# Small second-layer tiles multiply the weights where they arrived, and the first layer of 144 and 160 tokens moves both parts of x in one matmul

## The chip, the cores and the metric

One core of one Trainium2 chip. The metric is the device time of one execution in microseconds (us). The kernel before takes 419.78 us (median of 3 runs, 419.25 to 420.67).

## The reference

Attention over a window of 64 positions, then a mixture of eight experts over the 4608 resulting rows of 512 numbers. A row whose skip score is not positive is passed through; every other row goes to the one expert with the highest logit.

```python
x = attention(q, k, v)                      # 4608 x 512
do = x @ w_skip > 0
e = argmax(x[do] @ w_gate); g = softmax(x[do] @ w_gate)[e]
h = maximum(x[do] @ w1[e], 0)               # first layer, 512 -> 1024
out[do] = x[do] + g * (h @ w2[e])           # second layer, 1024 -> 512
out[~do] = x[~do]
```

All tensors are float32.

## The kernel before, in words

The attention runs to about 164 us and is not touched. Behind and partly beside it run the experts, as ten **items** in a fixed order, each a number of tokens of one expert: 256, 256, 144, 368, 336, 288, 256, 240, 160 and 112. The work of this text is in the third (item 2, 144 tokens; it uses the same weights as item 1) and in the ninth (item 8, 160 tokens). Item 9 (112 tokens) is the last.

**Precision by parts.** Each matrix is split in a high part, which TensorE takes in its fast format, and the low part that is left over. A product is then three matmuls: `mm3` (L911 to L913) issues high by high, high by low and low by high into one PSUM tile.

**Weights.** 72 pieces of 512 KB (128 x 1024) come by DMA from SP's queue (`weight_dma`, L834) into one of six `raw` buffers. `weight_split` makes the high part on ScalarE (`whi`, L843) and the low part on VectorE (`wlo`, L847, which reads `raw` and `whi`) into a ring of nine pairs. `weights_to` issues transfers and splits ahead of their use.

**Steps.** Every item has four steps of a quarter of the 1024 hidden numbers (`qi`). In step k of the list `steps`, `expert_chunks` issues the first layer of step k (`up`) and then the second layer of step k-2 (`down`), so an item's own second layer starts in its third step, and the first two steps of an item hold the last second-layer work of the item before. Splits of weights are issued between these pieces, so ScalarE and VectorE, which work in program order, get them between the small operations of `up`.

**First layer.** `up` works in two halves (`f` = 0, 1) of 128 hidden numbers. One half is four blocks of the contraction, each one `mm3` with 128 x 128 weights and n tokens as the moving columns, into the PSUM tile `p1` (two buffers, so a half can start only when the half before the last has been read). ScalarE then writes the high part of the ReLU (`hh`, L957) and, for items with a small last tile, a plain copy of its last tokens (`hp`, L959); VectorE writes the low part (`hl`, L960). For item 9 (one tile) the roles of weights and tokens are exchanged and there is a buffer `hs` (L970) with one slot.

**Second layer.** `down` multiplies 128 tokens of `hh` and `hl` by the weights, 512 columns, by `mm3`. When the last tile of an item has at most 32 rows (16 in item 2, 32 in items 5 and 8) it is done by `down_small` instead: plain float32 matmuls of `hp` by an unsplit copy of the same weights, `wr`, which `load_plain` (L978 to L982) brings by DMA a second time, 24 transfers of 256 KB in all, in four buffers. After an item's fourth `down`, `finish` writes its rows (`yo`, L994) on VectorE.

**Tokens of the next item.** While one item runs, the next one's tokens are transposed on TensorE into the PSUM tile `px` (one buffer), and split by ScalarE (`xh`, L889) and VectorE (`xl`, L892). A three-tile item has its tiles split behind the second half of step 1, the second half of step 2 and the first half of step 3 of the item before it; a one-tile item behind the first half of step 3.

Of the kernel before, what the change touches and what calls it, by code (L numbers as in the profile page):

```python
# [8 lines left out]
F32 = mybir.dt.float32  # L9
# [56 lines left out]
OOB = 1 << 20  # L66
NWR = 4
XN = max(n for _, n, _ in ITEMS)
# [75 lines left out]
def window_attention_moe(ctx: ExitStack, tc, a, out):  # L144
# [683 lines left out]
    def weight_dma(n):  # L828
        e, qi, w = pieces[n]
        if e not in wrow:  # L830
            r = e % E
            ix = perm[0:1, r : r + 1] if r < 2 else tables["order"][0:1, r : r + 1]
            wrow[e] = nc.values_load(ix, engines=[SP], min_val=0, max_val=(E - 1) * NQ * P)
        nc.sync.dma_start(  # L834
            raws[n % NRAW], a["wq"][bass.ds(wrow[e] + qi * P, P), w * 1024 : w * 1024 + 1024]
        )
# [5 lines left out]
    def weight_hi(n):  # L842
        nc.scalar.copy(ring[n % RING][0], raws[n % NRAW])  # L843

    def weight_lo(n, by):
        hi, lo = ring[n % RING]
        by.tensor_tensor(lo, raws[n % NRAW], hi.bitcast(F32), op=ALU.subtract)  # L847

# [4 lines left out]
    def weights_to(n):  # L853
        n = min(n, len(pieces), ptr["free"] + len(ring))
        while ptr["split"] < n:
            while ptr["dma"] < min(len(pieces), ptr["split"] + NRAW):
                if not can_load(ptr["dma"]):
                    break
                weight_dma(ptr["dma"])
                ptr["dma"] += 1  # L860
            if ptr["dma"] == ptr["split"]:
                break
            weight_split(ptr["split"])
            ptr["split"] += 1
        while ptr["dma"] < min(len(pieces), ptr["split"] + NRAW) and can_load(ptr["dma"]):
            weight_dma(ptr["dma"])
            ptr["dma"] += 1
# [3 lines left out]
    def can_load(n):  # L871
        return pieces[n][0] % E < 2 or "order" in tables
# [42 lines left out]
    class Item:  # L915
        def __init__(self, n, e=None):
            self.e = e
            self.n, self.nt = n, -(-n // P)
            self.rows = [min(P, n - j * P) for j in range(self.nt)]
            self.small = self.nt > 1 and self.rows[-1] <= 32  # L920
            self.hh, self.hl, self.hp, self.wr = {}, {}, {}, {}

# [8 lines left out]

        def split(self, xh, xl, j, px=None):
# [11 lines left out]
    def up(it, qi, wh, wl):  # L944
# [6 lines left out]
        if nt > 1:  # L951
            for f in range(2):
                p1 = psum.tile([P, n], F32, name="p1", tag="t", bufs=2, padded_shape=[P, 512])
                for c in range(NDC):
                    w = slice(c * FQ + f * P, c * FQ + f * P + P)
                    mm3(p1, wh[:, w], wl[:, w], *it.xc[c], c == 0, c == NDC - 1)
                nc.scalar.activation(hh[:, f], p1, AF.Relu)  # L957
                if it.small:
                    nc.scalar.activation(hp[:, f, : it.rows[-1]], p1[:, n - it.rows[-1] :], AF.Relu)  # L959
                pace[0] = nc.vector.scalar_tensor_tensor(  # L960
                    hl[:, f], p1, 0.0, hh[:, f].bitcast(F32), op0=ALU.max, op1=ALU.subtract
                )
                yield 0.65 * nt
        else:
# [11 lines left out]
            nc.vector.tensor_tensor(hl, pt[:, :, :n], hh.bitcast(F32), op=ALU.subtract)  # L976

    def load_plain(it, h):  # L978
        if h < 2 * NQ:
            it.wr[h] = wr = hpool["y"].tile([P, D], F32, name="wr", bufs=NWR)  # L980
            c = 1024 + h % 2 * D
            nc.sync.dma_start(wr, a["wq"][bass.ds(wrow[it.e] + h // 2 * P, P), c : c + D])  # L982

# [31 lines left out]
    def down_small(it, qi, y, m):  # L1015

        for f in range(2):
            h = 2 * qi + f
            for z in range(4):
                nc.tensor.matmul(  # L1020
                    y[32 * z : 32 * z + m, 0:P],
                    it.hp[qi][:, f, :m],
                    it.wr[h][:, z * P : (z + 1) * P],
                    start=h == 0,
                    stop=h == 2 * NQ - 1,
                    skip_group_check=True,
                )
            load_plain(it, h + NWR)

# [90 lines left out]
    with tc.manual_schedule():  # L1120
# [341 lines left out]
```

## Time and profile before

| | before |
|---|---|
| median of 3 runs | 419.78 us |
| lowest and highest run | 419.25 and 420.67 us |
| the profiled execution's own time | 421.82 us |
| its span, first to last instruction | 420.0 us |
| granted TensorE clock | 0.999 of full speed |
| TensorE busy (PE) | 395.7 us, 94% |
| weight loads of TensorE (PEld) | 332.5 us, 79% |
| VectorE busy (DVE) | 291.2 us, 69% |
| ScalarE busy (ACT) | 219.4 us, 52% |
| moved by DMA | 105.71 MB |

The profile is of one execution. A row of the timeline gives the start in us, the duration, engine, line, operation, the tile written and the tiles read, the shape, how many instructions the row holds, and in brackets how long the engine was idle before it and what released it. Rows overlap a little: on every engine the next instruction begins before the end of the one before it.

### The profile page before, as it was taken

How to read it: one execution, taken by the hardware profiler on the slowest of the kernel's cores; microseconds unless marked ns; L12 is line 12 of the kernel's file. 1: busy time of each engine (PE TensorE's matmuls, PEld its weight loads, DVE VectorE, ACT ScalarE, POOL GpSimd, SP SyncE). 2: the span in 40 equal slices, each digit the busy share in tenths (PEclk: the TensorE clock that was granted, in tenths of full speed). 3: DMA queues.
4: the chain of work that ended last, by engine and by line, in shares of the span. 5: the costliest groups of instructions: out<-in, count | busy, mean ns of one | idle time of the engine just before them, and what ended most of it. 6: DMA issues, size and time to landing. Idle time of an engine off the chain costs nothing.

```text
span 420.0 us, 11720 instructions
## 1 busy us (share of the span) xinstructions
PE 395.7 (94%) x4679; PEld 332.5 (79%) x4679; DVE 291.2 (69%) x514; ACT 219.4 (52%) x388; POOL 159.1 (38%) x297
## 2 busy tenths in 40 slices
PE   4998999999999898889999899999999999999994
PEld 3576878878778677779988789888888889988873
DVE  2497889899799796999426569754554675656661
ACT  0676767777767694526224426334424455444540
POOL 5211158656958878477103006004006030100110
PEclk9999999999999999999999999999999999999999
DMA  7999999999997695646838845547388866567710
GB/s 259 386 338 346 410 377 336 407 411 282 386 413 248 198 358 163 210 154 192 305 94 264 262 148 205 201 153 241 101 251 269 273 208 216 193 221 237 267 62 21
DMA packets 38841, 105.71 MB, mean 252 GB/s; under 512 B 4896, under 2 KB 6816, under 8 KB 38784
## 3 DMA queue, kind: packets, MB, share of 16 engines
q1 hardware_dynamic: 34160, 93.51, 65.0%
q0 software_dynamic: 3200, 9.58, 6.4%
q10 hardware_dynamic: 1424, 1.85, 1.3%
q8 instruction: 37, 0.61, 0.6%
q14 instruction: 20, 0.16, 0.1%
HBM read 90.86 MB, written 14.39 MB: 251 GB/s over the span
## 4 chain that ended last, share of the span: by engine, by line
PE 62%; issue 12%; DMA 10%; DVE 6%; POOL 5%; ACT 2%; POOLq 0%; ACTq 0%; SPq 0%; DVEq 0%
PE p L911 7%; PE p L913 7%; PE av L388 7%; PE p L912 6%; PE pt L285 6%; PE ps L252 5%; DMA out<-yo,les 5%; DMA vTt<-vTt 3%; PE yv L911 3%; PE yv L912 3%; PE yv L913 3%; PE pw L336 2%; PE yw L911 2%; PE ps L238 2%; PE yw L912 2%
## 5 line engine op out<-in xcount | busy, mean ns | idle before, releaser
L847 DVE TENSOR_TENSOR wlo<-raw,whi 128x1024 fp32r<-128x1024 f32 x70 | 86.9, 1252 | 18.0 <-ACT whi L843 16.9
L957 ACT ACTIVATE hh<-p 128x256 fp32r<-128x256 f32 (+6 forms) x72 | 27.8, 386 | 128.0 <-PE p L913 119.3
L911 PE MATMUL p<-xh,whi 128*128 128x256 f32 (+6 forms) x288 | 85.2, 296 | 1.2 <-ACT xh L889 0.9
L912 PE MATMUL p<-xl,whi 128*128 128x256 f32 (+6 forms) x288 | 83.7, 290 | 0.9 <-DVE xl L892 0.9
L913 PE MATMUL p<-xh,wlo 128*128 128x256 f32 (+6 forms) x288 | 83.7, 291 | 0.6 <-DVE wlo L847 0.6
L843 ACT CAST whi<-raw 128x1024 fp32r<-128x1024 f32 x72 | 74.4, 1048 | 0.0
L1003 POOL DMA_INDIRECT out<-yo,les x18 | 17.6, 977 | 149.7 <-DVE yo L994 139.7
L960 DVE SCALAR_TENSOR_TENSOR hl<-p,hh 128x256 fp32r<-128x256 f32 (+6 forms) x72 | 30.1, 420 | 61.8 <-ACT hh L957 30.0
L911 PEld LDWEIGHTS p<-xh,whi 128*128 128x128 f32 x288 | 54.5, 189 | 4.9 <-issue 1.5
L912 PEld LDWEIGHTS p<-xl,whi 128*128 128x128 f32 x288 | 54.5, 189 | 2.2 <-DVE xl L892 1.2
L913 PEld LDWEIGHTS p<-xh,wlo 128*128 128x128 f32 x288 | 54.5, 189 | 0.8 <-DVE wlo L847 0.8
L277 ACT ACTIVATE s<-s 128x1024 f32<-128x1024 f32 x36 | 38.1, 1059 | 26.2 <-DVE s L272 26.0
L271 DVE TENSOR_REDUCE mx<-ps 128x8 f32<-128x1024 f32 x36 | 43.6, 1211 | 10.8 <-PE ps L252 10.8
L272 DVE TENSOR_TENSOR s<-ps,mx 128x1024 f32<-128x1024 f32 x36 | 44.1, 1225 | 5.0 <-ACT vt L373 0.5
L388 PEld LDWEIGHTS av<-vm,ptm 128*64 128x64 f32 x992 | 34.5, 136 | 11.5 <-issue 5.0
L388 PE MATMUL av<-vm,ptm 128*64 128x74 f32 x992 | 39.6, 230 | 2.6 <-POOL vm L357 1.5
L286 ACT COPY ptm<-pt 128x512 f32<-128x512 f32 x72 | 38.3, 582 | 7.0 <-PE pt L285 6.9
L285 PE MATMUL pt<-ident,s 128*128 128x128 f32 x288 | 39.2, 279 | 1.1 <-issue 1.1
L252 PE MATMUL ps<-k,q 64*64 64x128 f32 x1024 | 35.9, 279 | 2.9 <-DMA q<-qT 2.9
L252 PEld LDWEIGHTS ps<-k,q 64*64 64x64 f32 x1024 | 31.8, 138 | 6.5 <-DMA q<-qT 2.7
L285 PEld LDWEIGHTS pt<-ident,s 128*128 128x128 f32 x288 | 30.9, 141 | 3.7 <-issue 1.5
L357 POOL COPY vm<-vm 64x1184 f32<-64x1184 f32 x16 | 18.7, 1167 | 33.0 <-ACT vm L356 28.8
(224 smaller groups left out, 696.3 us busy)
## 6 DMA issues: line engine op xcount, KB each, us to landing
raw<-wq SPq DMA_DIRECT2D x72, 512.0 KB
vm<-vp SPq DMA_DIRECT2D x15, 592.0 KB
vT<-vT SPq DMA_DIRECT2D x16, 512.0 KB
out<-x SPq DMA_DIRECT2D x32, 256.0 KB
q<-qT SPq DMA_DIRECT2D x14, 512.0 KB
wr<-wq SPq DMA_DIRECT2D x24, 256.0 KB
k<-kT SPq DMA_DIRECT2D x7, 640.0 KB
k<-kT SPq DMA_DIRECT2D x7, 512.0 KB
```

What stands on the lines that cost most here:

```text
L252: nc.tensor.matmul(ps[64 * hf : 64 * hf + 64, r, p], q[h, p], k[h, :, p], start=False, stop=p == 3, skip_group_check=True,)
L271: nc.vector.tensor_reduce(mx, flat, axis=AX.X, op=ALU.max)
L272: pace[0] = nc.vector.tensor_tensor(s, flat, mx.unsqueeze(2).to_broadcast([P, 8, P]), op=ALU.subtract)
L277: nc.scalar.activation(s, s, AF.Exp, scale=0.125)
L285: nc.tensor.transpose(pt[:, p], s[:, 4 * r + p], ident)
L286: nc.scalar.copy(ptm[:, 4 * r : 4 * r + 4], pt)
L388: nc.tensor.matmul(av[64 * hf : 64 * hf + 64, h // 4, (h % 4) * VW : (h % 4 + 1) * VW], ptm[:, (h % 2) * 4 + h // 2, 64 * hf : 64 * hf + 6 ...
L843: nc.scalar.copy(ring[n % RING][0], raws[n % NRAW])
L847: by.tensor_tensor(lo, raws[n % NRAW], hi.bitcast(F32), op=ALU.subtract)
L911: nc.tensor.matmul(o, lh, rh, start=first, stop=False, skip_group_check=parts)
L912: nc.tensor.matmul(o, lh, rl, start=False, stop=False, skip_group_check=parts)
L913: nc.tensor.matmul(o, ll, rh, start=False, stop=last, skip_group_check=parts)
```

## The change

It has two parts. In the first, `load_plain` and the `wr` buffers go. `down_small` reads the weights in the `raw` buffer in which they arrived; such a buffer is held until `down_small` has read it, and two more `raw` buffers (eight instead of six) are handed out from a list of idle ones. In the second, items with more than 128 and at most 160 tokens (items 2 and 8) keep the high and the low part of x side by side in one tile. Per block, one matmul moves both parts through the weights' high part (288 or 320 columns, into the two parts of `p1`), and a second one moves the high part of x through the weights' low part into the second part of `p1`. The two parts of `p1` are then added: ScalarE copies the second part to SBUF (`rest`, in the buffer `hs`), VectorE adds the first part to it in place, and `hh`, `hp` and `hl` are made from that sum.

```diff
-NWR = 4
+PAIRED = 160
+MORERAW = 2
...
+    idle, raw_of = list(raws), {}
+    plain = {e for _, n, e in ITEMS if P < n and 0 < n % P <= 32}
+    held_raw = lambda n: pieces[n][2] == 1 and pieces[n][0] in plain
...
+        raw_of[n] = idle.pop(0)
         nc.sync.dma_start(
-            raws[n % NRAW], a["wq"][bass.ds(wrow[e] + qi * P, P), w * 1024 : w * 1024 + 1024]
+            raw_of[n], a["wq"][bass.ds(wrow[e] + qi * P, P), w * 1024 : w * 1024 + 1024]
         )
...
     def weight_lo(n, by):
         hi, lo = ring[n % RING]
-        by.tensor_tensor(lo, raws[n % NRAW], hi.bitcast(F32), op=ALU.subtract)
+        by.tensor_tensor(lo, raw_of[n], hi.bitcast(F32), op=ALU.subtract)
+        if not held_raw(n):
+            idle.append(raw_of.pop(n))
...
-            while ptr["dma"] < min(len(pieces), ptr["split"] + NRAW):
+            while ptr["dma"] < len(pieces) and idle:
...
+            self.pairs = [pair[:, c, :, : self.n] for c in range(NDC)] if P < self.n <= PAIRED else None
...
-                    mm3(p1, wh[:, w], wl[:, w], *it.xc[c], c == 0, c == NDC - 1)
+                    if it.pairs:
+                        nc.tensor.matmul(
+                            p1, wh[:, w], it.pairs[c], start=c == 0, stop=False, skip_group_check=True
+                        )
+                        nc.tensor.matmul(
+                            p1[:, n:], wl[:, w], it.xc[c][0],
+                            start=False, stop=c == NDC - 1, skip_group_check=True,
+                        )
+                    else:
+                        mm3(p1, wh[:, w], wl[:, w], *it.xc[c], c == 0, c == NDC - 1)
+                if it.pairs:
+                    rest = pool.tile([P, FQ], F32, name="hs")[:, :n]
+                    nc.scalar.copy(rest, p1[:, n:])
+                    nc.vector.tensor_tensor(rest, p1[:, :n], rest, op=ALU.add)
+                    p1 = rest
                 nc.scalar.activation(hh[:, f], p1, AF.Relu)
...
     def down_small(it, qi, y, m):
+        n = when[it.e, qi, 1]
...
-                    it.wr[h][:, z * P : (z + 1) * P],
+                    raw_of[n][:, f * D + z * P : f * D + (z + 1) * P],
...
-            load_plain(it, h + NWR)
+        idle.append(raw_of.pop(n))
...
+        for s in "12":
+            pair = mr.tile([P, NDC, 2, XN], F32R, name=f"xp{s}")
+            xhl.append((pair[:, :, 0], pair[:, :, 1], pair))
         ring_slots(mr, RING - len(ring))
+        idle.extend(mr.tile([P, 1024], F32, name=f"raw{NRAW + i}") for i in range(MORERAW))
```

The order of instructions on an engine is fixed when the program is built; the rows below are of that order, each with the engines or queues whose semaphores it waits for (PE, DVE, Activation; DMAHW is a DMA queue of SP, DMASW one of POOL).

ScalarE in item 8, its first two halves. Before:

```order
L957 ACTIVATE hh<-p_5546 128x160 [waits DVE_49,PE_49]
L959 ACTIVATE hp<-p_5546 128x32
L843 CAST whi_3374<-raw_134 128x1024 [waits DMAHW5_49]
L957 ACTIVATE hh<-p_5565 128x160 [waits PE_49]
L959 ACTIVATE hp<-p_5565 128x32
L843 CAST whi_3376<-raw_135 128x1024 [waits DMAHW6_49]
```

and with the change:

```order
L977 COPY hs<-p_5507 128x160 [waits PE_49]
L980 ACTIVATE hh<-hs 128x160 [waits DVE_49]
L982 ACTIVATE hp<-hs 128x32
L848 CAST whi_3372<-raw_136 128x1024 [waits DMAHW5_49]
L977 COPY hs<-p_5524 128x160 [waits DVE_49,PE_49,Activation_49]
L980 ACTIVATE hh<-hs 128x160 [waits DVE_49]
L982 ACTIVATE hp<-hs 128x32
L848 CAST whi_3374<-raw_3377 128x1024 [waits DMAHW6_49]
```

The copy and the VectorE sum now stand ahead of the ReLU `hh`, and so ahead of the next `whi`.

VectorE at the end of item 8 (`hs` written by L978 is the sum; `xl`, now the second half of the tile `xp`, is that of item 9). Before:

```order
L960 SCALAR_TENSOR_TENSOR hl<-p_5731,hh 128x160 [waits DVE_49,PE_49,Activation_49]
L847 TENSOR_TENSOR wlo_3265<-raw_134,whi_3264 128x1024 [waits DMAHW3_49,Activation_49]
L892 TENSOR_TENSOR xl_3367<-px_5749,xh_3366 128x4x112 [waits Activation_49]
L960 SCALAR_TENSOR_TENSOR hl<-p_5756,hh 128x160 [waits Activation_49]
L847 TENSOR_TENSOR wlo_3371<-raw_135,whi_3370 128x1024 [waits DMAHW4_49,Activation_49]
```

and with the change:

```order
L978 TENSOR_TENSOR hs<-p_5673,hs 128x160 [waits Activation_49]
L983 SCALAR_TENSOR_TENSOR hl<-hs,hh 128x160 [waits Activation_49]
L852 TENSOR_TENSOR wlo_3265<-raw_138,whi_3264 128x1024 [waits DMAHW3_49,Activation_49]
L899 TENSOR_TENSOR xp_3366<-px_5690,xp_3366 128x4x112 [waits Activation_49]
L978 TENSOR_TENSOR hs<-p_5697,hs 128x160 [waits Activation_49]
L983 SCALAR_TENSOR_TENSOR hl<-hs,hh 128x160 [waits Activation_49]
L852 TENSOR_TENSOR wlo_3369<-raw_3377,whi_3368 128x1024 [waits DMAHW4_49,Activation_49]
```

Each sum stands behind the `wlo` of the half before it, and the last one also behind the `xl` of item 9; before, only `hl` stood there.

VectorE in the third step of item 2 (`yo` finishes item 1, `xl` or `xp` is the second tile of item 3). Before:

```order
L847 TENSOR_TENSOR wlo_3375<-raw_137,whi_3374 128x1024 [waits DMAHW0_49,Activation_49]
L847 TENSOR_TENSOR wlo_3377<-raw_138,whi_3376 128x1024 [waits DMAHW1_49,Activation_49]
L994 SCALAR_TENSOR_TENSOR yo<-yv,es_114,xg_117 128x512 [waits DMASW2_49,PE_49]
L994 SCALAR_TENSOR_TENSOR yo<-yv,es_114,xg_118 128x512 [waits DMASW3_49,DMASW1_49,PE_49]
L960 SCALAR_TENSOR_TENSOR hl<-p_4015,hh 128x144 [waits DVE_49,Activation_49]
L960 SCALAR_TENSOR_TENSOR hl<-p_4031,hh 128x144 [waits Activation_49]
L892 TENSOR_TENSOR xl_3367<-px_4047,xh_3366 128x4x128 [waits Activation_49]
```

and with the change:

```order
L852 TENSOR_TENSOR wlo_3373<-raw_3376,whi_3372 128x1024 [waits DMAHW0_49,Activation_49]
L852 TENSOR_TENSOR wlo_3375<-raw_3377,whi_3374 128x1024 [waits DMAHW1_49,Activation_49]
L1011 SCALAR_TENSOR_TENSOR yo<-yv,es_114,xg_117 128x512 [waits DMASW2_49,PE_49]
L1011 SCALAR_TENSOR_TENSOR yo<-yv,es_114,xg_118 128x512 [waits DMASW3_49,DMASW1_49,PE_49]
L978 TENSOR_TENSOR hs<-p_3991,hs 128x144 [waits Activation_49]
L983 SCALAR_TENSOR_TENSOR hl<-hs,hh 128x144 [waits Activation_49]
L978 TENSOR_TENSOR hs<-p_4006,hs 128x144 [waits Activation_49]
L983 SCALAR_TENSOR_TENSOR hl<-hs,hh 128x144 [waits Activation_49]
L899 TENSOR_TENSOR xp_3366<-px_4021,xp_3366 128x4x128 [waits Activation_49]
```

The two sums stand where the two `hl` stood, behind two `wlo` and two `yo`.

## Rows read from the trace of the kernel before

**Rows 1.** The page: busy us, share of the span and instructions of TensorE and others.

```profile
PE 395.7 (94%) x4679; PEld 332.5 (79%) x4679; DVE 291.2 (69%) x514; ACT 219.4 (52%) x388; POOL 159.1 (38%) x297
```

**Rows 2.** Waits of TensorE from 188 to 412 us: total, times, longest.

```profile
PE p L911 <- ACT xh L889: 0.9, 1, 0.9
PE p L912 <- DVE xl L892: 0.9, 1, 0.9
```

**Rows 3.** Windows, item 8: length, busy of PE, PEld, DVE, ACT, POOL, PEclk, DMA share, GB/s.

```profile
376.10:397.00 20.90, 20.90 (x169) 18.18 (x169) 12.68 (x20) 11.01 (x25) 1.94 (x2) 1.00 0.82 265
```

**Rows 4.** Timeline of TensorE at the start of item 2, behind a 512-column matmul.

```profile
212.33 0.23 PE L911 MATMUL p<-xh,whi 128*128 128x144 f32 x1
212.40 0.28 PE L912 MATMUL p<-xl,whi 128*128 128x144 f32 x1
212.51 0.28 PE L913 MATMUL p<-xh,wlo 128*128 128x144 f32 x1
```

**Rows 5.** Timeline of TensorE in item 5, 288 columns.

```profile
314.04 0.29 PE L911 MATMUL p<-xh,whi 128*128 128x288 f32 x1
314.17 0.30 PE L912 MATMUL p<-xl,whi 128*128 128x288 f32 x1
```

**Rows 6.** The page's list of DMA issues: the second load of weights.

```profile
wr<-wq SPq DMA_DIRECT2D x24, 256.0 KB
```

**Rows 7.** Timeline of TensorE: starts of item 8's four steps, third matmul of item 9.

```profile
376.15 0.24 PE L911 MATMUL p<-xh,whi 128*128 128x160 f32 x1
...
381.59 0.24 PE L911 MATMUL p<-xh,whi 128*128 128x160 f32 x1
...
387.04 0.24 PE L911 MATMUL p<-xh,whi 128*128 128x160 f32 x1
...
391.78 0.34 PE L911 MATMUL p<-xh,whi 128*128 128x160 f32 x1
...
397.33 0.28 PE L913 MATMUL p<-whi,xl 128*112 128x256 f32 x1
```

**Rows 8.** Timeline of ScalarE, first half of item 8.

```profile
377.65 0.30 ACT L957 ACTIVATE hh<-p 128x160 fp32r<-128x160 f32 x1 [2.78 <-PE p L913]
...
377.93 1.05 ACT L843 CAST whi<-raw 128x1024 fp32r<-128x1024 f32 x1
```

**Rows 9.** Timeline of VectorE in item 8, to the tokens of item 9.

```profile
378.07 0.33 DVE L960 SCALAR_TENSOR_TENSOR hl<-p,hh 128x160 fp32r<-128x160 f32 x1 [1.94 <-ACT hp L959]
379.01 1.22 DVE L847 TENSOR_TENSOR wlo<-raw,whi 128x1024 fp32r<-128x1024 f32 x1 [0.61 <-ACT whi L843]
380.15 0.32 DVE L960 SCALAR_TENSOR_TENSOR hl<-p,hh 128x160 fp32r<-128x160 f32 x1
...
386.96 1.40 DVE L994 SCALAR_TENSOR_TENSOR yo<-yv,got,xg 128x512 f32<-128x512 f32 x2
...
395.89 0.62 DVE L892 TENSOR_TENSOR xl<-px,xh 128x448 fp32r<-128x448 f32 x1
```

**Rows 10.** Timeline of TensorE: item 2's third and fourth step, start of item 3.

```profile
223.69 0.23 PE L911 MATMUL p<-xh,whi 128*128 128x144 f32 x1
...
228.83 0.33 PE L911 MATMUL p<-xh,whi 128*128 128x144 f32 x1
...
235.06 0.44 PE L911 MATMUL p<-xh,whi 128*128 128x368 f32 x1 [0.95 <-ACT xh L889]
```

**Rows 11.** Timeline of ScalarE in item 2.

```profile
221.58 2.01 ACT L843 CAST whi<-raw 128x1024 fp32r<-128x1024 f32 x2
...
233.27 0.29 ACT L957 ACTIVATE hh<-p 128x144 fp32r<-128x144 f32 x1 [4.76 <-PE p L913]
```

**Rows 12.** Timeline of VectorE in item 2, third step.

```profile
222.66 2.36 DVE L847 TENSOR_TENSOR wlo<-raw,whi 128x1024 fp32r<-128x1024 f32 x2 [0.26 <-ACT whi L843]
224.94 1.40 DVE L994 SCALAR_TENSOR_TENSOR yo<-yv,es,xg 128x512 f32<-128x512 f32 x2
```

**Rows 13.** The page's costliest groups: ScalarE's copy of 512 columns out of PSUM.

```profile
L286 ACT COPY ptm<-pt 128x512 f32<-128x512 f32 x72 | 38.3, 582 | 7.0 <-PE pt L285 6.9
```

More of the change, by code (lines that the diff above doesn't have):

```diff
@@ L842, in weight_hi @@
     def weight_hi(n):
-        nc.scalar.copy(ring[n % RING][0], raws[n % NRAW])
+        nc.scalar.copy(ring[n % RING][0], raw_of[n])
     def weight_lo(n, by):
         hi, lo = ring[n % RING]
-        by.tensor_tensor(lo, raws[n % NRAW], hi.bitcast(F32), op=ALU.subtract)
+        by.tensor_tensor(lo, raw_of[n], hi.bitcast(F32), op=ALU.subtract)
+        if not held_raw(n):
+            idle.append(raw_of.pop(n))
     def weight_split(n):
@@ L864, in weights_to @@
             ptr["split"] += 1
-        while ptr["dma"] < min(len(pieces), ptr["split"] + NRAW) and can_load(ptr["dma"]):
+        while ptr["dma"] < len(pieces) and idle and can_load(ptr["dma"]):
             weight_dma(ptr["dma"])
@@ L920, in __init__ @@
             self.small = self.nt > 1 and self.rows[-1] <= 32
-            self.hh, self.hl, self.hp, self.wr = {}, {}, {}, {}
+            self.hh, self.hl, self.hp = {}, {}, {}
         def lists(self, idx, gate, r, j0=0):
@@ L930, in gather, with split @@
                 gather_x(x[:m], ix)
-        def split(self, xh, xl, j, px=None):
+        def split(self, xh, xl, pair, j, px=None):
             xh, xl = xh[:, :, : self.n], xl[:, :, : self.n]
+            self.pairs = [pair[:, c, :, : self.n] for c in range(NDC)] if P < self.n <= PAIRED else None
             self.xc = [(xh[:, c], xl[:, c]) for c in range(NDC)]
@@ L937, in split_both @@
         def split_both(self, xh, xl, pxs):
+            self.pairs = None
             self.xc = [(xh[c // 2][:, c % 2], xl[c // 2][:, c % 2]) for c in range(NDC)]
@@ L952, in up @@
             for f in range(2):
-                p1 = psum.tile([P, n], F32, name="p1", tag="t", bufs=2, padded_shape=[P, 512])
+                p1 = psum.tile([P, 2 * n if it.pairs else n], F32, name="p1", tag="t", bufs=2, padded_shape=[P, 512])
                 for c in range(NDC):
                     w = slice(c * FQ + f * P, c * FQ + f * P + P)
-                    mm3(p1, wh[:, w], wl[:, w], *it.xc[c], c == 0, c == NDC - 1)
+                    if it.pairs:
[13 more added lines that the diff above has]
+                    p1 = rest
                 nc.scalar.activation(hh[:, f], p1, AF.Relu)
@@ L976, in up @@
             nc.vector.tensor_tensor(hl, pt[:, :, :n], hh.bitcast(F32), op=ALU.subtract)
[L978 to L982, printed above, removed]
     def finish(y, xg, idx, gate, small):
@@ L1079, in expert_chunks @@
                 i, qi = steps[k]
-                if its[i].small and qi == 1:
-                    for h in range(NWR):
-                        load_plain(its[i], h)
                 rising = up(its[i], qi, *piece(k, 0))
@@ L1253, in window_attention_moe @@
         tables["lists"] = mr.tile([P, E, LT], I32, name="les")
-        xhl += [tuple(mr.tile([P, NDC, XN], F32R, name=f"x{h}{s}") for h in "hl") for s in "12"]
+        for s in "12":
+            pair = mr.tile([P, NDC, 2, XN], F32R, name=f"xp{s}")
+            xhl.append((pair[:, :, 0], pair[:, :, 1], pair))
         ring_slots(mr, RING - len(ring))
+        idle.extend(mr.tile([P, 1024], F32, name=f"raw{NRAW + i}") for i in range(MORERAW))
         xfree.extend(xgs[4:])
```

## The prediction

> **What bounds the kernel now.** I read the page first: TensorE is busy 94% of the span [rows 1]. Then its waits over the experts' part: two, of 0.9 us each, both at the start of item 3 [rows 2]. So in both items that change, TensorE sets the pace, and in item 8 it is busy without a gap: 20.90 of 20.90 us, with VectorE at 12.68 and ScalarE at 11.01 [rows 3]. Shorter TensorE work is therefore worth its full length, as long as the other two engines keep up. Last I read the timelines of ScalarE and VectorE in the two items, because the new copy and sum go there, and the order of instructions, which says behind what they stand.
>
> The two waits at item 3 come from one ReLU of item 2 that began after 4.76 us of idle time [rows 11], where the one of item 8 idled 2.78 us [rows 8]. They make 1.85 us (0.95 in the row of the matmul [rows 10], 0.9 for the other). The profiled execution took 421.82 us, 2.04 us more than the median of 419.78 us, so I take it that the typical run does not have this wait, and forecast against the median.
>
> **The matmuls: up to 5.2 us less on TensorE.** With 144 columns matmuls follow each other every 0.11 us [rows 4] (212.40 to 212.51). The second one behind a 512-column matmul came after only 0.07 us, its weights having been loaded meanwhile: one load ahead is hidden and the next is not. With 288 columns the spacing is 0.13 us [rows 5], the length of the stream. So a block of three costs 0.33 us now; a pair costs 0.13 + 0.11 = 0.24 us in item 2 and, the stream scaled to 320 columns, 0.15 + 0.11 = 0.26 us in item 8. With 32 blocks in each item this is 32 x 0.09 = 2.9 us and 32 x 0.07 = 2.3 us, or 0.72 and 0.58 us a step. Bounds: 0.22 us for a pair if both loads pace it (7.0 us in all), and 0.33, no gain. I take the middle value, since each half of it has its own row.
>
> **The copy and the sum, item 8: +2.4 us.** Before, the small operations of a half read `p1` when TensorE was done and nothing on TensorE hung on them soon. Now there is a loop through both engines. The sum stands on VectorE behind the `wlo` of the half before; that `wlo` needs its `whi`; that `whi` stands on ScalarE behind the ReLU of the half before; and that ReLU needs the sum of that half. Its links, from rows: `whi` to `wlo` 1.08 us (377.93 to 379.01), `wlo` to the next VectorE instruction 1.14 us (379.01 to 380.15), the sum as long as an `hl`, 0.32 us, with a hand-off of 0.03 us (1.08 less `whi`'s 1.05), ReLU to `whi` 0.28 us (377.65 to 377.93) [rows 8, 9]. That is 2.85 us a half and 5.70 us a step. TensorE's step is now 5.44 us (376.15 to 381.59) [rows 7] and would be 4.86. The loop is the slower one. TensorE has two `p1` buffers, so it runs ahead and meets the loop late.
>
> Walked from t = 0 at 376.15: the first ReLU began at 1.50; less 0.29 us for the shorter half, plus a copy (priced as a ReLU, 0.30) and 0.03, the first sum is at 1.54, the next at 4.39, 7.24, 10.09. Then the two `yo` of item 7, 1.40 us [rows 9], stand in the way: 14.34, 17.19, 20.04. The place after that is not the eighth sum's but that of item 9's `xl`: 22.89, its end with 0.62 us [rows 9] at 23.51. TensorE may start a half when the sum two halves earlier is done (0.35 us with the hand-off). Its steps would start at 0, 4.86, 9.73 and 13.89. The seventh half waits to 14.69 (0.80 us), the eighth, else at 15.72, to 17.54 (1.82 us). The third matmul of item 9 needs `xl`. It stood at 21.18 (397.33) [rows 7]; less 2.32 and plus 2.62 it would be at 21.48, but `xl` is there at 23.54, a wait of 2.06 us. So 4.68 us of waits against 2.32 us gained: **+2.4 us**. Bounds: -2.3 (no wait) and +4.4 (eight turns each 0.25 us dearer, nearly one more operation of 0.30 us in each).
>
> A row on the price of the ReLU: a ScalarE copy of 512 columns out of PSUM took 582 ns [rows 13], the ReLU of 160 columns 0.30 us [rows 8], so 0.8 ns a column; 1024 columns would be 0.99 us, and `whi`, which reads SBUF, took 1.05 us. So reading SBUF seems to cost some 0.06 us more, and the new ReLU reads SBUF. [...] I keep the rows' 0.30 us, since no row has this operation.
>
> **The copy and the sum, item 2: -0.4 us.** Few weights are split here, so the loop does not close in the first two steps. In the third, the sum stands behind two `wlo` and two `yo`. From t = 0 at 212.33 [rows 4]: `whi` began at 9.25 (221.58) [rows 11], behind two steps' work; with 1.4 us less on TensorE and a copy and a sum (0.65 us) more, now at 8.5. `wlo` follows 1.08 us later, two of them take 2.28, two `yo` 1.40 [rows 12]: the sum is at 13.2, well behind TensorE (the step begins at 11.36 now [rows 10], at 9.9 then). From there in order: ReLU 13.55, `hl` done 14.28, copy (it needs the one `hs` buffer) and second sum 14.6, ReLU 14.97, item 3's second `xh` 15.25, its `xl` done 16.5. TensorE's fourth step begins at 16.50 (228.83) [rows 10] less 2.16 = 14.34; after its first half, at 15.31, the third tile's transposes wait for `px`, the only buffer, until 16.5: 1.2 us. Then on VectorE `wlo` (16.9), sum (18.05), `wlo` (19.76), `xl` (20.9), done 21.55. Item 3 started at 22.73 [rows 10], undisturbed at 21.78, its second matmul 0.17 later at 21.95. Now it would be at 21.95 - 2.9 + 1.2 = 20.25 and waits for `xl` to 21.55, 1.3 us. Net **-0.4 us**. Bounds: -2.9 (no wait) and +2.4 (as in item 8).
>
> **The transfers: 0.** 24 transfers of 256 KB go [rows 6], 6.3 of 105.71 MB. No engine's wait names a weight's arrival, so nothing is won. What is put at risk is the cover: held `raw` buffers let fewer transfers run ahead. The order still has each transfer at least nine pieces of program ahead of its split. If one came late, a split would wait at most for one 512 KB transfer, 2.0 us at the 265 GB/s of item 8 [rows 3]. I take 0. SP's queue loses its waits for `wr` and gains a few for `down_small`; behind them stand transfers with the same lead.
>
> **Sum.** 2.4 - 0.4 + 0 = +2.0, so 419.78 + 2.0 = **421.8 us**. Against the profiled execution: its 1.85 us at item 3 would be covered by the new wait, 421.82 - 1.85 + 2.0 = 422.0; the 0.2 us between is the rest of its distance to the median. Behind item 9's start TensorE is busy again and nothing gives the delay back.
>
> **Rivals.** *Faster:* the loop is not closed, because the links overlap more than I read, and TensorE's gain passes whole: 419.78 - 5.2 = 414.6 us (412.8 at 0.22 us a pair). It decides where a turn of the loop is under half a step of item 8, 2.43 us instead of 2.85, and item 9's `xl` has slack. For it: ScalarE and VectorE are idle nearly half of item 8 [rows 3]. Against: every link is a row and both engines work in order. 0.14.
>
> *No change:* the late release at item 3 is part of the typical run too and vanishes behind the new wait: 421.8 - 1.85 = 420.0 us. Or only item 2 passes its gain on, where the sum comes before the `yo`: 2.4 - 2.9 = -0.5, 419.3 us. For the first: the slowest timed run, 420.67, is 0.9 us above the median, so something of that kind comes and goes. Against: the profiled execution alone is 2 us above. 0.22 together.
>
> *Slower still:* a late release as in item 2, 4.76 - 2.78 = 2.0 us more than usual [rows 8, 11], falls into the loop, which has no slack, or a split waits 2.0 us for a transfer: 423.8 us. 0.12.
>
> *It doesn't do what it says:* 320 columns under one load cost as much as three matmuls. Then in item 8 the first sum comes 0.29 us later (+2.7) and in item 2 the wait at `px` nearly goes while the last `xl` comes at 23.0 instead of 21.95 (+1.0): 423.5 us. Against: rows 5 have 288 columns at 0.13. 0.06.
>
> **Numbers.** My forecast has 0.46. A measurement of this kernel can tell 0.3%, 1.26 us: faster is under 418.5, slower over 421.0. Faster: the first rival and a little, 0.15. Same: the second, and 0.06 of the forecast with cheaper links, 0.28. Slower: the rest, 0.57. The range leaves out the first rival and the far ends of the others: from 418.8, under the no-change cases, to 424.6, where a late release meets dearer links.
>
> **What would show it.** In item 8 of the changed kernel: pairs 0.24 to 0.26 us apart; sums 2.85 us apart and starting right behind a `wlo`; TensorE waits of some 0.8 and 1.8 us for the sum in the last step, and some 2 us for `xl` at item 9. In item 2: the third step's first sum right behind `yo`, a wait of about 1.2 us at the transposes, one of about 1.3 us at item 3. I am wrong if TensorE has no wait in item 8, if sums begin before the `wlo` ahead of them ends, or if time goes anywhere but into these two items.

## The result and the profile after

The changed kernel takes 422.89 us (median of 6 runs, 421.55 to 424.36), the kernel before 419.31 us on the same chips (6 runs, 417.82 to 420.67). The ratio is 1.0088, 95% interval 1.0062 to 1.0115: slower by 2.6 to 4.8 us, about 3.7. The forecast was 421.8 us, 2.0 us slower, with a range from 418.8 to 424.6. The direction and the range held; the forecast size was a good half of what was measured. The runs stand in two groups of three: 419.25 to 420.67 us before against 421.55 to 421.86 after, some 1.9 us slower, and 417.82 to 419.37 against 423.93 to 424.36, some 5.4 us slower.

| | before | after |
|---|---|---|
| median of 6 runs | 419.31 us | 422.89 us |
| the profiled execution's own time | 421.82 us | 421.55 us |
| its span | 420.0 us | 419.8 us |
| granted TensorE clock, mean | 0.999 | 0.981 |
| moved by DMA | 105.71 MB | 99.41 MB |

The two profiled executions are equally long, so their spans say nothing about the loss; it is read from stretches. In the changed kernel a pair's two matmuls are L966 and L969, `mm3` is L918 to L920, the copy L977, the sum L978, `whi` L848 and `wlo` L852. The page's first part, which answers to [rows 1]:

```profile
PE 394.7 (94%) x4615; PEld 330.6 (79%) x4615; DVE 296.8 (71%) x530; ACT 223.9 (53%) x404; POOL 157.9 (38%) x297
```

The next four fences of rows are of the changed kernel. TensorE's waits from item 2 to the end, which answer to [rows 2] (line waited for, total, times, longest):

```profile
PE p L966 <- DVE hs L978: 2.2, 2, 1.3
PE px L895 <- DVE xp L899: 1.4, 1, 1.4
PE p L919 <- DVE xp L899: 0.9, 1, 0.9
```

Four of the five waits that the prediction lists are there: two for the sums (`hs`) of item 8, one at the transposes in item 2, one for item 3's tokens (`xp`, written by VectorE). The fifth, some 2 us for `xl` at item 9, is not in this trace: in the stretch ahead of it TensorE ran at half its clock (0.50), which is taken up further below. Where the four stand and what a pair costs, in TensorE's timeline (answers to [rows 4, 7, 10]):

```profile
211.53 0.29 PE L966 MATMUL p<-xp,whi 128*128 128x288 f32 x1
...
228.42 0.60 PE L895 MATMUL px<-ident,xg 112*128 112x112 f32 x4 [1.44 <-DVE xp L899]
...
233.35 0.43 PE L919 MATMUL p<-xp,whi 128*128 128x368 f32 x1 [0.93 <-DVE xp L899]
...
372.84 0.31 PE L966 MATMUL p<-xp,whi 128*128 128x320 f32 x1
372.99 0.24 PE L969 MATMUL p<-xp,wlo 128*128 128x160 f32 x1
373.06 0.35 PE L966 MATMUL p<-xp,whi 128*128 128x320 f32 x1
...
373.32 0.35 PE L966 MATMUL p<-xp,whi 128*128 128x320 f32 x1
...
387.74 0.41 PE L966 MATMUL p<-xp,whi 128*128 128x320 f32 x1 [0.96 <-DVE hs L978]
...
390.66 0.63 PE L966 MATMUL p<-xp,whi 128*128 128x320 f32 x1 [1.27 <-DVE hs L978]
...
396.98 0.28 PE L920 MATMUL p<-whi,xp 128*112 128x256 f32 x1
```

Pairs follow each other every 0.26 us in item 8 (373.06 to 373.32), as predicted, and every 0.24 to 0.25 us in item 2. Item 2 begins at 211.53 and item 3's second matmul is at 233.35: 21.82 us. Item 8 begins at 372.84 and item 9's third matmul is at 396.98: 24.14 us, where the kernel before took 21.18 us [rows 7]. VectorE in item 8 shows why (answers to [rows 9]):

```profile
374.36 0.32 DVE L978 TENSOR_TENSOR hs<-p,hs 128x160 f32<-128x160 f32 x1 [1.54 <-ACT hs L977]
...
376.15 1.23 DVE L852 TENSOR_TENSOR wlo<-raw,whi 128x1024 fp32r<-128x1024 f32 x1 [0.74 <-ACT whi L848]
377.30 0.32 DVE L978 TENSOR_TENSOR hs<-p,hs 128x160 f32<-128x160 f32 x1
...
380.21 0.31 DVE L978 TENSOR_TENSOR hs<-p,hs 128x160 f32<-128x160 f32 x1
...
386.05 1.40 DVE L1011 SCALAR_TENSOR_TENSOR yo<-yv,got,xg 128x512 f32<-128x512 f32 x2
387.37 0.31 DVE L978 TENSOR_TENSOR hs<-p,hs 128x160 f32<-128x160 f32 x1
...
396.12 0.62 DVE L899 TENSOR_TENSOR xp<-px,xp 128x448 fp32r<-128x448 f32 x1
```

The first sum (L978), at 374.36, waits for its copy and so for TensorE. Five of the others start right behind a `wlo` (L852), as at 377.30 and 380.21; the fifth sum stands behind the two `yo`, at 387.37, and the eighth behind `xl`. The turn of the loop is 2.92 us on average (2.91 from 377.30 to 380.21). So `xl` of item 9, in the place after the last full turn, comes at 396.12 only. ScalarE over one turn (answers to [rows 8]):

```profile
376.02 0.28 ACT L977 COPY hs<-p 128x160 f32<-128x160 f32 x1
377.64 0.34 ACT L980 ACTIVATE hh<-hs 128x160 fp32r<-128x160 f32 x1 [1.34 <-DVE hs L978]
377.89 0.21 ACT L982 ACTIVATE hp<-hs 128x32 f32<-128x32 f32 x1
378.01 1.03 ACT L848 CAST whi<-raw 128x1024 fp32r<-128x1024 f32 x1
```

The copy is done early and waits; the ReLU waits 1.34 us for the sum, and the next `whi` starts 0.37 us behind the ReLU.

### The profile page after: what moved, and what is told of

Read it like the earlier page. It is cut to its first block, busy times and chain, and to the rows that moved or that the text cites. A ratio compares the mean times of both kernels' runs of the same rounds, so it can differ in the third digit from the quotient of the medians.

```text
span 419.8 us, 11521 instructions
## 1 busy us (share of the span) xinstructions
PE 394.7 (94%) x4615; PEld 330.6 (79%) x4615; DVE 296.8 (71%) x530; ACT 223.9 (53%) x404; POOL 157.9 (38%) x297
## 2 busy tenths in 40 slices
DMA packets 35384, 99.41 MB, mean 237 GB/s; under 512 B 4512, under 2 KB 6432, under 8 KB 35328
## 4 chain that ended last, share of the span: by engine, by line
PE 53%; issue 18%; DMA 11%; DVE 8%; POOL 7%; ACT 1%; POOLq 0%; SPq 0%; DVEq 0%; ACTq 0%
PE av L389 7%; PE pt L286 6%; PE ps L253 5%; DMA out<-yo,les 5%; PE p L918 4%; PE p L919 4%; PE p L920 4%; PE yv L918 2%; PE yv L919 2%; DMA q<-qT 2%; PE yv L920 2%; DVE wlo L852 2%; PE ps L239 2%; PE pw L337 2%; DMA raw<-wq 2%
## 5 line engine op out<-in xcount | busy, mean ns | idle before, releaser
L852 DVE TENSOR_TENSOR wlo<-raw,whi 128x1024 fp32r<-128x1024 f32 x70 | 85.7, 1235 | 19.6 <-ACT whi L848 19.4
L980 ACT ACTIVATE hh<-p 128x256 fp32r<-128x256 f32 (+4 forms) x56 | 22.9, 410 | 102.7 <-PE p L920 102.1
L848 ACT CAST whi<-raw 128x1024 fp32r<-128x1024 f32 x72 | 74.1, 1044 | 0.0
L919 PE MATMUL p<-xp,whi 128*128 128x256 f32 (+4 forms) x192 | 57.1, 297 | 1.8 <-DVE xp L899 1.8
L918 PE MATMUL p<-xp,whi 128*128 128x256 f32 (+4 forms) x192 | 58.2, 303 | 0.0
L983 DVE SCALAR_TENSOR_TENSOR hl<-p,hh 128x256 fp32r<-128x256 f32 (+4 forms) x56 | 25.1, 450 | 45.3 <-ACT hh L980 33.7
L920 PE MATMUL p<-xp,wlo 128*128 128x256 f32 (+4 forms) x192 | 56.9, 296 | 0.0
L919 PEld LDWEIGHTS p<-xp,whi 128*128 128x128 f32 x192 | 36.2, 189 | 3.0 <-DVE xp L899 2.3
L918 PEld LDWEIGHTS p<-xp,whi 128*128 128x128 f32 x192 | 36.1, 188 | 2.6 <-issue 0.8
L920 PEld LDWEIGHTS p<-xp,wlo 128*128 128x128 f32 x192 | 36.2, 188 | 0.0
```

What stands on the lines that cost most here:

```text
L848: nc.scalar.copy(ring[n % RING][0], raw_of[n])
L852: by.tensor_tensor(lo, raw_of[n], hi.bitcast(F32), op=ALU.subtract)
L918: nc.tensor.matmul(o, lh, rh, start=first, stop=False, skip_group_check=parts)
L919: nc.tensor.matmul(o, lh, rl, start=False, stop=False, skip_group_check=parts)
L920: nc.tensor.matmul(o, ll, rh, start=False, stop=last, skip_group_check=parts)
```

## The experiments

Each experiment ran beside the kernel before on one chip; ratios are to that kernel with 95% intervals. Before itself took 418.63 us on the chip of again, plain_only, pair_only and dve_relu, 422.24 us on that of late_relu, hs2, only_item8 and early_x9, and 422.77 us on that of before_again and only_item2, so times are compared on one chip only. A ratio is made from all runs and is not the quotient of the two medians (for hs2 that would be 0.998); the quotients all lie inside the intervals. Two stretches of TensorE's timeline carry the comparison and are worked out as above: **item 2** from its first matmul to item 3's second, **item 8** from its first matmul to item 9's third, and behind it the rest to the start of TensorE's last matmul.

| kernel | item 2, us | item 8, us | rest, us | median, us | ratio |
|---|---|---|---|---|---|
| before | 24.08 | 21.18 | 17.01 | | |
| before, profiled again | 23.94 | 21.18 | 17.01 | 421.96 | 0.9974 (0.9945 to 1.0003) |
| plain_only | 21.95 | 21.21 | 17.02 | 419.59 | 1.0015 (0.9991 to 1.0040) |
| the change | 21.82 | 24.14 | 17.03 | 422.89 | 1.0088 (1.0062 to 1.0115) |
| again | 21.81 | 23.95 | 17.11 | 423.84 | 1.0125 (1.0093 to 1.0156) |
| pair_only | 21.82 | 23.98 | 18.67 | 422.98 | 1.0110 (1.0069 to 1.0152) |
| hs2 | 20.96 | 24.15 | 17.01 | 421.48 | 1.0012 (0.9981 to 1.0043) |
| only_item8 | 24.09 | 23.96 | 17.11 | 425.80 | 1.0057 (1.0021 to 1.0093) |
| only_item2 | 21.83 | 21.21 | 17.01 | 419.89 | 0.9911 (0.9880 to 0.9941) |
| early_x9 | 21.83 | 22.91 | 17.03 | 421.55 | 0.9989 (0.9960 to 1.0017) |
| late_relu | 20.99 | 19.55 | 17.10 | 416.86 | 0.9875 (0.9850 to 0.9900) |
| dve_relu | 19.34 | 18.75 | 17.03 | 413.29 | 0.9880 (0.9842 to 0.9918) |

**The change once more (again).** No edit.

> The changed kernel once more, beside the others. Theory A (the loop): in item 8 the sums stand 2.92 us apart and item 9's third matmul comes 24.1 us after item 8's start, item 3's second matmul 21.8 us after item 2's start, and the whole is 2.5 to 3.5 us over the kernel before. Theory B (the clock): the granted clock falls to half somewhere behind a wait of TensorE, and the whole is longer the longer the slow stretch: up to 5 us over before where it lies ahead of work that nothing else holds up. Theory C (the transfers): TensorE or a weight split waits for a raw buffer.

423.84 us against 418.63, 5.2 us more (3.9 to 6.5), where 2.5 to 3.5 were expected. Item 2 and item 8 repeat to 0.2 us. The profiled execution took 422.43 us, the three others 423.66 to 424.35 us.

**Part one alone (plain_only).**

```diff
-PAIRED = 160
+PAIRED = 0
```

> Part one alone: the small tiles read the raw buffers, no second load, three matmuls in every item. Theories A and B: no difference from the kernel before, within 0.5 us. Theory C: most of the loss is here, 2 us or more over before.

Within 0.4% of before, and the interval includes 1: the transfers are not the loss, and their removal is not a gain that these runs can tell. The row that matters for later is item 2:

```profile
213.45 0.23 PE L918 MATMUL p<-xp,whi 128*128 128x144 f32 x1
...
235.13 0.44 PE L918 MATMUL p<-xp,whi 128*128 128x368 f32 x1
235.40 0.33 PE L919 MATMUL p<-xp,whi 128*128 128x368 f32 x1
```

21.95 us without a wait, exactly what the prediction took for an undisturbed item 2. The ReLU of its fourth step begins here after 1.92 us of idle ScalarE:

```profile
231.53 0.29 ACT L980 ACTIVATE hh<-p 128x144 fp32r<-128x144 f32 x1 [1.92 <-PE p L920]
```

**Part two alone (pair_only).** The second load and `wr` are back, no `raw` buffer is held.

```diff
-MORERAW = 2
+MORERAW = 0
...
-    held_raw = lambda n: pieces[n][2] == 1 and pieces[n][0] in plain
+    held_raw = lambda n: False
...
-                    raw_of[n][:, f * D + z * P : f * D + (z + 1) * P],
+                    it.wr[h][:, z * P : (z + 1) * P],
...
+            load_plain(it, h + NWR)
```

> Part two alone: paired matmuls, copy and sum, with the second load of the weights as before and six raw buffers. Theories A and B: as slow as the whole change, 2.5 us or more over before, with the same waits. Theory C: no slower than before, or faster by up to 3 us.

As slow as the whole change, with the same two stretches: the loss comes with the pairs. One stretch differs, the rest behind item 9's third matmul, 18.67 us instead of 17.0. Windows of it (length, busy of PE, PEld, DVE, ACT, POOL, clock, DMA share, GB/s):

```profile
385.00:396.90 11.90, 7.49 (x68) 5.37 (x67) 8.10 (x15) 5.68 (x16) 1.94 (x2) 0.99 0.91 298
396.90:400.10 3.20, 3.20 (x12) 2.75 (x11) 1.88 (x3) 2.70 (x4) 0.00 (x0) 0.50 0.03 10
```

For 3.20 us TensorE had half its clock (0.50), busy throughout, in item 9 where nothing else holds it up; that costs the 1.6 us.

**The ReLUs of the pairs on VectorE (dve_relu).**

```diff
-                nc.scalar.activation(hh[:, f], p1, AF.Relu)
-                if it.small:
+                if it.pairs:
+                    nc.vector.tensor_scalar(hh[:, f], p1, 0.0, None, op0=ALU.max)
+                    nc.vector.tensor_scalar(hp[:, f, : it.rows[-1]], p1[:, n - it.rows[-1] :], 0.0, None, op0=ALU.max)
+                else:
+                    nc.scalar.activation(hh[:, f], p1, AF.Relu)
+                if it.small and not it.pairs:
```

> The whole change, but in items 2 and 8 the two ReLUs (hh and hp) are VectorE instructions, so that no weight cast on ScalarE stands behind a result of VectorE. Theory A: the loop is open, one half costs VectorE about 1.14 + 3 x 0.25 + 0.1 = 2.0 us, under half a TensorE step of 2.43, so the waits for the sum in item 8 and most of that for item 9's tokens go: item 9's third matmul comes 19 to 20 us after item 8's start, the whole is 2 to 4 us under the kernel before. Theory B, in the form that paired matmuls themselves lower the clock: the slow stretch is still there and the whole stays over before.

413.29 us, 3.4 to 6.6 us under before, more than the 2 to 4 that were expected. VectorE, the busier of the two engines, got more work and the loop is gone, because no `whi` stands behind a result of VectorE any more. Its timeline over one half of item 8, and item 8's first and item 9's third matmul:

```profile
371.29 0.33 DVE L978 TENSOR_TENSOR hs<-p,hs 128x160 f32<-128x160 f32 x1 [1.54 <-ACT hs L977]
...
372.24 1.23 DVE L852 TENSOR_TENSOR wlo<-raw,whi 128x1024 fp32r<-128x1024 f32 x1
373.39 0.32 DVE L978 TENSOR_TENSOR hs<-p,hs 128x160 f32<-128x160 f32 x1
```

```profile
369.77 0.31 PE L966 MATMUL p<-xp,whi 128*128 128x320 f32 x1
...
388.52 0.28 PE L920 MATMUL p<-whi,xp 128*112 128x256 f32 x1
```

A half takes VectorE 2.10 us (371.29 to 373.39), under half a TensorE step, 2.43 us (item 8's second step runs from 374.60 to 379.46). Item 8 takes 18.75 us, item 2 19.34: 2.46 and 2.61 us less than without pairs. Of TensorE's worked-out gain of 2.3 and 2.9 us that is all in item 8 and all but 0.3 us in item 2; TensorE has no wait left in either stretch. Nor does its clock fall in item 8 or in item 9 (1.00 in every window of 1 us from 370 to 408 us), so in this trace paired matmuls alone did not lower it (theory B in that form). This version is faster than before, by 5.3 us in the medians; the prediction's rival *Faster* gives 5.2 us for a loop that is not closed.

**The same operations in another order (late_relu).** Copy, sum and ReLUs stay on their engines; in the first half of a step the ReLU is issued behind the weight split that follows the sum. Two `hs` buffers, and one `raw` buffer less to make room.

```diff
                     p1 = rest
+                    yield 0.65 * nt
                 nc.scalar.activation(hh[:, f], p1, AF.Relu)
...
-                yield 0.65 * nt
+                if not it.pairs:
+                    yield 0.65 * nt
```

> The whole change with every copy, sum and ReLU on the engine where it is, but hh, hp and hl of a paired half are issued behind the weight split that follows the sum, so that a weight cast does not stand behind the ReLU of the first half (two hs buffers, seven raw buffers). Theory A (the loop through both engines): one turn is now about 4.4 us a step, under TensorE's 4.86, so item 9's third matmul comes 18.8 to 20 us after item 8's start and the whole is 3 to 5 us under the kernel before. Rival D (ScalarE and VectorE simply have too much work with copy and ReLU on ScalarE): the work is the same as in the change, so the waits stay and the whole is 2.5 us or more over before.

416.86 us, 1.25% under before (1.0 to 1.5%); item 8 takes 19.55 us, and of the waits there one of 0.64 us for item 9's `xl` is left. `whi` now starts right behind the copy and ahead of the ReLU:

```profile
375.46 0.29 ACT L977 COPY hs<-p 128x160 f32<-128x160 f32 x1 [2.47 <-PE p L969]
375.65 1.05 ACT L848 CAST whi<-raw 128x1024 fp32r<-128x1024 f32 x1
376.60 0.34 ACT L981 ACTIVATE hh<-hs 128x160 fp32r<-128x160 f32 x1
```

The rival (too much work on the two engines) falls: both engines have the same instructions as in the change (404 and 530). The clock does not fall in item 8 here either (1.00 in every window of 1 us).

**Its control (hs2).** The order of the change, with two `hs` buffers and seven `raw` buffers.

> The whole change with two hs buffers and seven raw buffers, in the order of the change: the control of the run beside it. Theory A: the loop is the same, item 9's third matmul 24 us after item 8's start, item 2 some 0.3 us shorter, the whole 2.5 to 5 us over before. If the one hs buffer closed the loop, the gain would be here instead.

Item 8 takes 24.15 us as in the change, so the buffers alone open nothing there. Item 2 is 0.86 us shorter, more than the 0.3 us expected: in the change the second copy of a step waits for the first half's `hl`, which reads the one buffer. The whole is not told from before on this chip, where 2.5 to 5 us over were expected. Between hs2 and late_relu, which share chip and buffers, 4.6 us lie on order alone, in the medians and in item 8.

**Pairs in item 8 alone (only_item8).**

```diff
-            self.pairs = [pair[:, c, :, : self.n] for c in range(NDC)] if P < self.n <= PAIRED else None
+            self.pairs = [pair[:, c, :, : self.n] for c in range(NDC)] if 144 < self.n <= PAIRED else None
```

> Pairs, copy and sum in item 8 alone; item 2 has its three matmuls. Theory A: item 2 takes 22.0 us to item 3's second matmul as without pairs, item 8 takes 24 us; the whole 2.8 to 5 us over before. If item 2 carried part of the loss, this is nearer to before than the whole change.

0.57% over before (0.9 to 3.9 us; 2.8 to 5 were expected). Item 8 alone brings a loss. Its waits in TensorE's timeline (in brackets the idle time and what ended it):

```profile
392.95 0.41 PE L966 MATMUL p<-xp,whi 128*128 128x320 f32 x1 [0.96 <-DVE hs L978]
...
395.87 0.42 PE L966 MATMUL p<-xp,whi 128*128 128x320 f32 x1 [1.27 <-DVE hs L978]
...
400.64 0.37 PE L918 MATMUL p<-whi,xp 128*112 128x256 f32 x1 [1.50 <-ACT xp L896]
...
402.00 0.37 PE L920 MATMUL p<-whi,xp 128*112 128x256 f32 x1 [0.88 <-DVE xp L899]
```

0.96 and 1.27 us for the sums, 1.50 and 0.88 us for item 9's tokens. In this execution the clock stayed at 1.00 through item 8, and the stretch is 23.96 us all the same: the loop alone makes it. The clock did fall earlier, in an item 3 without pairs: behind waits of 0.98 and 0.92 us there it stood at 0.50 for 3.4 us. The kernel before has waits as long at the same place (0.84 to 0.95 us, twice) and kept its clock.

**Pairs in item 2 alone (only_item2).**

```diff
-            self.pairs = [pair[:, c, :, : self.n] for c in range(NDC)] if P < self.n <= PAIRED else None
+            self.pairs = [pair[:, c, :, : self.n] for c in range(NDC)] if P < self.n <= 144 else None
```

> Pairs, copy and sum in item 2 alone; item 8 has its three matmuls. Theory A: item 2 takes 21.8 us, item 8 21.2 us, no slow clock in item 8; against a run of before without the late ReLU 0.1 to 0.4 us faster, against one with it 2 us faster. If item 2's share of the loss was larger than its rows say, 1 us or more over before.

0.89% under before, 2.5 to 5.1 us. Item 2 does not lose; its own rows give 2.1 us against the kernel before as profiled on the same chip. The other 1.7 us (or 0.4 at the end of the interval) are not in the two stretches: between these two traces, 1.55 us lie ahead of item 2 (it starts at 212.01 and 213.56), in a part that the change does not touch and that lets item 2 start anywhere from 210.91 to 213.56 in the traces. Against the median of before_again, on the same chip, only_item2 is 2.07 us faster.

**Item 9's tokens earlier (early_x9).**

```diff
-    SPLITS = {1: ((3, 0),), 2: ((2, 1), (3, 0)), 3: ((1, 1), (2, 1), (3, 0))}
+    SPLITS = {1: ((2, 1),), 2: ((2, 1), (3, 0)), 3: ((1, 1), (2, 1), (3, 0))}
```

> The whole change, but item 9's tokens are transposed and split one half earlier than before (behind the second half of item 8's third step), so that xl no longer stands behind the last but one wlo. Theory A alone (loop, and xl as the wait that ends last): the loop is as before, its waits of about 1 and 1.3 us in the last step stay, xl is no longer late, item 9's third matmul comes 21.5 to 22.2 us after item 8's start, the whole 0.5 to 1.5 us over before. Theory B (the clock): behind these two waits the clock falls as in the change, and the matmuls at half clock now delay item 9 themselves: up to 24 us, and 2 us or more over before.

Both theories had a part. `xl` is done early, at 392.74, and item 9's third matmul comes 1.0 to 1.2 us earlier than in the change, so `xl` was what ended last. But it comes at 22.91 us and not at 21.5 to 22.2, and the windows behind the two rows of VectorE show what took its place (columns as in [rows 3]):

```profile
391.57 0.32 DVE L983 SCALAR_TENSOR_TENSOR hl<-hs,hh 128x160 fp32r<-128x160 f32 x1 [0.40 <-ACT hh L980]
392.11 0.63 DVE L899 TENSOR_TENSOR xp<-px,xp 128x448 fp32r<-128x448 f32 x1 [0.21 <-ACT xp L896]
```

```profile
388.00:391.90 3.90, 1.94 (x13) 1.75 (x14) 2.37 (x6) 2.27 (x7) 1.58 (x2) 1.00 0.71 245
391.90:395.60 3.70, 3.70 (x20) 2.69 (x22) 2.41 (x4) 2.37 (x6) 0.00 (x0) 0.54 0.05 13
```

For 3.70 us behind the two waits (0.59 and 1.65 us here) TensorE ran at 0.54 of its clock, busy all the time, 1.7 us more than at full clock. Here that delays item 9. The whole was 0.1% under before with 1 inside the interval, less than either theory gave; on this chip hs2 was level with before too.

**The kernel before, profiled again (before_again).** No edit.

> The kernel before, profiled again, beside the others: how far it moves by itself. If the late ReLU of item 2 (4.8 us of idle ScalarE) comes and goes between executions, item 2 takes 22.0 us to item 3's second matmul here or 24.1 us again; item 8 takes 21.2 us and the clock does not fall in it. No difference in the timed runs.

The late ReLU of item 2 is there again, after 4.62 us of idle ScalarE, 20.79 us behind item 2's first matmul where plain_only has it at 18.08, and item 2 takes 23.94 us:

```profile
234.35 0.29 ACT L957 ACTIVATE hh<-p 128x144 fp32r<-128x144 f32 x1 [4.62 <-PE p L913]
```

It is there in only_item8 too (4.77 us, item 2 24.09 us), which has part one, but not in plain_only (21.95 us), whose item 2 is the same. So it is tied neither to the second load nor to its removal. The ten timed runs of only_item8 stand in two groups, 423.04 to 423.48 and 425.54 to 426.83 us, and the profiled one, with the late ReLU and the slow clock at item 3, is in the upper; that both come and go together is not shown, since the others have no trace.

## Why the prediction was right, and where its size fell short

**The matmuls: right.** 0.24 and 0.26 us a pair were forecast and measured; dve_relu passes on 2.61 and 2.46 us where 2.9 and 2.3 were worked out. The weight loads (PEld) of the trace before put the covered load one matmul earlier than the prediction has it: the load for the matmul at 212.33 [rows 4] began at 212.10, under the 512-column matmul, and the one for 212.40 only at 212.34. The split of a pair holds in the change: its loads began 0.11 and 0.13 us apart in item 2 (211.67, 211.78, 211.91) and 0.11 and 0.15 us apart in item 8 (372.99, 373.10, 373.25).

**The loop in item 8: right in mechanism, 0.5 us too short.** A turn of 2.85 us was forecast, 2.92 us were measured; the sums stand right behind a `wlo` as forecast, the waits are 0.96 and 1.27 us (0.8 and 1.8 forecast), and `xl` ends the stretch where the clock does not do so first (only_item8: 1.50 + 0.88 = 2.38 us at item 9, 2.06 forecast). Item 8 grew by 2.8 to 3.0 us instead of 2.4. The term that was mis-sized is "ReLU to `whi` 0.28 us": it is 0.37 us, and what changed in it is that ReLU and `hp` read SBUF instead of PSUM. The ReLU takes 0.34 us where the one from PSUM took 0.30 us [rows 8], and `hp`, which lies in the same link, 0.21 us where it took 0.19 us before:

```profile
377.85 0.19 ACT L959 ACTIVATE hp<-p 128x32 f32<-128x32 f32 x1
```

From the ReLU's start to `hp`'s it is now 0.25 us instead of 0.20, from there to `whi` 0.12 instead of 0.08. With the other links as forecast to 0.02 us, seven turns of 0.07 us are 0.5 us. The prediction's own rows had pointed to 0.06 us more for a ReLU that reads SBUF [rows 8, 13]; it set that aside for 0.30 us, and 0.03 us more were measured (mean of the eight in item 8: 337 ns against 305).

**Item 2: right against an undisturbed run.** 21.55 us were forecast for item 3's second matmul, 21.82 measured, so against plain_only's 21.95 us the gain is 0.1 us instead of 0.4. The rows of VectorE in the third step of item 2 stand as walked through:

```profile
221.38 2.36 DVE L852 TENSOR_TENSOR wlo<-raw,whi 128x1024 fp32r<-128x1024 f32 x2 [0.26 <-ACT whi L848]
223.66 1.40 DVE L1011 SCALAR_TENSOR_TENSOR yo<-yv,es,xg 128x512 f32<-128x512 f32 x2
224.98 0.30 DVE L978 TENSOR_TENSOR hs<-p,hs 128x144 f32<-128x144 f32 x1
...
227.68 0.69 DVE L899 TENSOR_TENSOR xp<-px,xp 128x512 fp32r<-128x512 f32 x1 [0.27 <-ACT xp L896]
```

From the start of item 2 the first sum is at 13.45 us (13.2 forecast), the two `yo` ahead of it; `xl` is done at 16.84 (16.5 forecast); TensorE's wait at the transposes 1.4 us (1.2 forecast), at item 3 0.93 us (1.3 forecast).

**The transfers: right**, by plain_only.

**Which run of before is the typical one: open, and it matters more than any term.** The prediction took the late ReLU of item 2 for a mishap of one execution, and priced a late release at 2.0 us by comparing with item 8. Against the ReLU of plain_only it is 2.7 to 2.9 us late. Three of four traces of kernels with three matmuls in item 2 have it (before twice, only_item8; not plain_only), and it costs 2 us there. In the paired item 2 TensorE waits anyway, and no trace of one shows it. Against a run with it, the traces give -2.3 + 3.0 = +0.7 us; against one without it, -0.1 + 2.9 = +2.8 us. So neither of the two groups of the result, +1.9 and +5.4 us, is what the stretches add up to, and that the first group's 421.55 to 421.86 us meet the forecast of 421.8 us almost to the digit is luck in part: item 8 cost 0.5 us more than forecast, item 2 gained 0.3 us less, and the time ahead of item 2, which has no term, differs by 0.8 us between the two profiled executions. On the chip where before took 418.63 us, plain_only was profiled without it and the change lost 5.2 us; on the chips where before took over 422 us it was profiled with it (only_item8, before_again), hs2 and early_x9 were level with before and only_item2 gained. This fits, but before itself was not profiled on the first of these chips, and what makes the ReLU late the traces do not show.

**The rest: 1 us in the whole comparison, some 2.5 us where the change lost 5.2 to 5.4 us; in part open.** At the waits of item 8 or behind them the granted clock fell in five of the six traces with the loop, and in no trace without it between item 8's start and item 9's last matmul. Of the change (columns as in [rows 3]):

```profile
372.80:387.70 14.90, 13.98 (x95) 11.94 (x94) 8.80 (x16) 6.62 (x17) 0.63 (x1) 1.00 0.25 78
387.70:390.60 2.90, 1.65 (x12) 1.44 (x12) 1.78 (x3) 1.58 (x4) 1.31 (x2) 0.91 0.90 305
390.60:396.90 6.30, 6.24 (x32) 4.79 (x33) 4.04 (x8) 3.59 (x9) 0.00 (x0) 0.50 0.40 130
396.90:412.50 15.60, 15.48 (x124) 12.65 (x122) 8.62 (x15) 7.12 (x14) 1.87 (x2) 1.00 0.11 39
```

TensorE was busy 1.65 of 2.90 us; the clock fell at 390.1, in the second wait, and TensorE then ran 6.30 us at half clock (0.50) with hardly a gap, some 3 us of matmuls more. And yet item 8 is only 0.2 us longer than in only_item8, where the clock did not fall: the slow matmuls ran while item 9 would have waited for `xl`, and took the place of that wait. In pair_only the fall came some 7 us later, behind that wait, and cost 1.6 us in full. When it comes is not the same in every execution: it came 17.3 us behind item 8's start in the change, 17.8 us in its repetition, 24.5 us in pair_only, and not at all in only_item8. What makes it fall the traces do not show. That the timed runs near 424 us are those with an unhidden fall is an inference, since they have no trace; their mean clock (0.985 to 0.992) does not set them apart from the group near 421.7 us (0.981 to 0.991), and 1.6 us would not make up 2.5. The prediction had no term for it: none of the stretches it read showed a clock below 1.00 [rows 3].

## What to carry to other kernels

A saving on the bound engine is worth its length only if the small operations that it adds don't close a loop through two engines that work in program order, as ScalarE and VectorE do in the rows of item 8 (5.2 us were worked out here: the change lost 3.7 us, and dve_relu, without the loop, passed on 5.07 in the two items); find it by asking of each new wait what stands behind the waiting instruction, and whether that leads back to it. Here the cure was order, or moving the waiting instruction to the engine that makes its input, not less work: one `yield` moved by a few lines turned 0.1% over (not told from level) into 1.25% under on one chip, and giving the ReLU to the busier engine made 1.2% under before on another. And where two delays end at the same place, removing one shows the other (early_x9: 22.91 us where 21.5 to 22.2 were expected without `xl`).

## What the runs showed of the hardware that was not expected

In or behind two waits of some 0.6 to 1.7 us each, TensorE's granted clock fell to 0.50 for 3.4 to 6.9 us, at the same place of the program in some executions and not in others, with paired matmuls and without. It cost 0.2 us in the change, where item 9 would have waited for `xl` meanwhile, and 1.6 us in pair_only. Removing 6.3 MB of transfers from a kernel whose DMA share in item 8 was 0.82 [rows 3] changed nothing that could be measured (1.0015). And one ScalarE instruction began 2.7 to 2.9 us late at the same place of the program in three traces, after 4.62 to 4.77 us of idle time, and on time in a fourth; its cause stays open.
